# Float16 attention weights from tile 3 on in a fused top-k attention and two-MLP kernel

## The chip, the cores and the metric

One core of a Trainium2 chip runs the whole kernel. The metric is device time in microseconds (us). The engines are TensorE (PE; its weight loads are PEld), VectorE (DVE), ScalarE (ACT), GpSimd (POOL) and SyncE (SP), whose queue issues every DMA here.

## What is computed

```python
# q, k, v: (2, 8, 576, 64) float32; top_k = 32
scores = scale * np.matmul(q, k.transpose(0, 1, 3, 2))
kth = np.partition(scores, -top_k, axis=-1)[..., -top_k:-top_k + 1]
scores = np.where(scores >= kth, scores, -1000000000.0)
attn = np.exp(scores - np.max(scores, axis=-1, keepdims=True))
attn = attn / (np.sum(attn, axis=-1, keepdims=True) + 1e-09)
x = np.matmul(attn, v)            # then (2*576, 8*64) = (1152, 512) tokens
h = x @ moe_w_in                  # (512, 2048)
x = np.maximum(0.01 * h, h) @ moe_w_out
h = x @ moe2_w_in
out = (h * np.tanh(np.log1p(np.exp(np.minimum(h, 20.0))))) @ moe2_w_out   # softplus = h above 20
```

## The kernel before

The 1152 tokens are nine tiles of 128. Tiles 0 to 3 lie in batch 0, tile 4 half in each batch, tiles 5 to 8 in batch 1. A slot is one head of one tile; the 72 slots run one after the other, and the work of many stages is written into the same loop under priorities (`at`): a planner orders each engine's instructions by priority and by its own simulated times.

Float32 data that must keep its precision is split into two float16 halves, high and low, after scaling by a power of two (`pow2`). Keys, queries, activations and the four weight matrices are always split; products are then three matmuls (high×low, low×high, high×high).

A slot's steps: scores on TensorE, in two halves of 288 columns, both by way of the one bank of `ps_s`, each copied by ScalarE (`front`, two slots ahead of the rest); the top 32 by VectorE, four `max` and three `match_replace` (`topk`); masking and exponentials by ScalarE, L509 and L510 (`weigh`); then the weights, transposed, times the values (`back`).

`back` has two routes. In tiles below T16 = 5 it is float32: four transposes on TensorE into the bank `ps_pt`, a copy by ScalarE, a fifth transpose of the last 64 columns, a copy, five products. From tile 5 on `back16` runs: ScalarE casts the weights to the high half (L542), GpSimd subtracts to get the low half (L543), one transposing DMA on SP's queue turns ten blocks of 128 columns (L546), and 15 float16 matmuls multiply them by the split values (L553 to L555). Its halves `eh` stand in two buffers in turn, its transposed blocks `pts` in a buffer of the value pool `kvp`, which has VB = 5: four pairs of values and this one.

Values are loaded raw per pair of heads; `split_v` scales and splits a pair in place: squares, a scaled copy and a cast on ScalarE, a subtraction on GpSimd, two times. Before, only batch 1's pairs are split, from slot 34 on, after tile 4 has used them in float32. Its scratch `asides` and the one of `eh` lie in the scratch end of the weight arena `warena`, used until the 16 quarters of MLP weights are prepared (slots 0 to 16).

The MLP's steps (`Layer`, `product_in`, `product_out`) are spread over the slots with LEAD = 5 slots of lower priority; what is left runs after slot 71. The 16 quarters are loaded and split in the first slots (`load_w`, `split_w`).

Of the kernel before, what the change touches and what calls it, by code (L numbers as in the profile page):

```python
# [18 lines left out]
def topk_attention_moe_moe2_kernel(  # L19
# [34 lines left out]
    VB = 5  # L54
    LV = 0
# [4 lines left out]
    qp = ctx.enter_context(tc.tile_pool(name="qp", bufs=1))  # L60
# [243 lines left out]
    def load_kv(src, pool, tag, b, hp):  # L304
# [5 lines left out]
        for to, at0, n in (((0, S - P, P),) if src is k else ((0, S - SREM, SREM), (SREM, S - P, P - SREM))):  # L310
            nc.sync.dma_start(out=t[to:to + n, :, 4, :],
                              in_=src[b, 2 * hp:2 * hp + 2, at0:at0 + n, :].rearrange("h p d -> p h d"))
# [78 lines left out]
    def prep_q(t, qr):  # L391
# [5 lines left out]
        for c in range(2):  # L397
            if by_dma:
                qn = ksp.tile([P, 2, S], F16, tag="kst", name="qn").rearrange("p a b -> p (a b)")[:, :8 * P]
            else:  # L400
                qn = qp.tile([P, 4, 3, D], F16, tag="qn", name="qn").rearrange("p a b c -> p (a b c)")
# [36 lines left out]
    class Tile_:  # L438
# [11 lines left out]
        def front(self, h):  # L450
# [11 lines left out]
            for half in range(2):  # L462
                where, tag = ((ps_s, "s"), (ps_pt, "pt"))[half if self.t >= SB else 0]
# [48 lines left out]
        def back(self, h):  # L512
# [9 lines left out]
            where, tag = ((ps_pt, "pt"), (ps_g, "g"))[self.t >= TG]  # L522
            pu = where.tile([P, 512], F32, tag=tag, name="pu")
# [8 lines left out]
        def back16(self, h, e):  # L532

            hp, hh = divmod(h, 2)
            if not ehs:
                ehs.append(wh[:, 4 * NCHW * 2 * CH:4 * NCHW * 2 * CH + 2 * SP].rearrange("p (c n) -> p c n", c=2))
                t = krp.tile([P, 2, NB, D], F32, tag="kr", name="eh")
                ehs.append(t.rearrange("p a b c -> p (a b c)").bitcast(F16).rearrange("p (c n) -> p c n", c=2))
                for eh in ehs:
                    nc.gpsimd.memset(eh[:, :, S:], 0.0)  # L540
            eh = ehs[h % 2]
            nc.scalar.copy(eh[:, 0, :S], e)  # L542
            nc.gpsimd.tensor_tensor(out=eh[:, 1, :S], in0=e, in1=eh[:, 0, :S], op=ALU.subtract)  # L543
            pts = kvp.tile([P, 2, NB, D], F32, tag="kv", name="pts")
            ph = pts.rearrange("p a b c -> p (a b c)").bitcast(F16).rearrange("p (n q) -> p n q", q=P)
            nc.sync.dma_start(out=ph, in_=eh.rearrange("p c n -> p (c n)"), transpose=True)  # L546
            for b, s, n, p0 in tokens(self.t):
                o = self.av[p0:p0 + n, h * D:(h + 1) * D]
                for i, r in enumerate(R):
                    first, last = i == 0, i == NB - 1  # L550
                    pa, pb = [ph[:r, c * NB + i, p0:p0 + n] for c in range(2)]
                    va, vb = [vsp[b, hp][:r, hh, c, i, :] for c in range(2)]
                    nc.tensor.matmul(o, lhsT=pa, rhs=va, start=first, stop=False)  # L553
                    nc.tensor.matmul(o, lhsT=pa, rhs=vb, start=False, stop=False)
                    nc.tensor.matmul(o, lhsT=pb, rhs=va, start=False, stop=last)  # L555
# [44 lines left out]
    def product_in(m, hi, lo, g, t):  # L600
        where, tag = ((ps_m, "m"), (ps_pt, "pt"))[t >= MB and g == 3]
# [51 lines left out]
    class Layer:  # L653
# [11 lines left out]
        def first(self, g):  # L665
            ph = product_in(2 * self.l, self.hi, self.lo, g, self.t)
# [113 lines left out]
    T16 = 5  # L780
    TG = 5
    VS = 98
    VX = 34
# [3 lines left out]
    SB = 99  # L787
    YB = 99
    MB = 7
# [38 lines left out]
    for i in range(-2, NS):  # L828
# [27 lines left out]
        if i % 2 == 0:  # L856
            for bp in ((0, (i - VS) // 2), (1, (i - VX) // 2)):
                if bp in vst and bp not in vsp and T16 < NTT:
                    split_v(*bp)
# [7 lines left out]
    n = NS  # L867
    while todo or late:
# [33 lines left out]
```

## Time and profile before

| what | us |
|---|---|
| median of 3 runs (731.74 to 733.25) | 732.8 |
| the profiled execution's own time | 732.71 |
| its span, first to last instruction | 730.9 |
| mean granted TensorE clock, share of full | 0.962 |

The profile is of one execution; its span lies 1.8 us below that execution's time.

### The profile page before, as it was taken

The page shows a single profiled execution, that of the slowest core. Times are in us where ns is not written, and L with a number is a line of the kernel's source. Part 1 is how long each engine was busy: PE and PEld are TensorE (multiplying, and loading weights), DVE is VectorE, ACT ScalarE, POOL GpSimd, SP SyncE. Part 2 cuts the span into 40 slices and gives each one's busy share as a digit, 9 for nine tenths or more (in the row PEclk, how much of TensorE's full clock was granted, in tenths as well). Part 3 has the DMA queues.
Part 4 walks back from the last instruction along what each step waited for, and adds up shares of the span by engine and source line. Part 5 has one row for each costly group of instructions (what it writes and reads, how often), then busy time and mean ns, then how long its engine had stood idle before and what let it go on. Part 6 is the DMA issues. An engine that isn't in the chain of part 4 may idle for free.

```text
span 730.9 us, 16578 instructions
## 1 busy us (share of the span) xinstructions
PE 645.2 (88%) x6428; PEld 464.6 (64%) x6428; DVE 561.2 (77%) x1184; ACT 541.1 (74%) x1056; POOL 394.0 (54%) x550
## 2 busy tenths in 40 slices
PE   2389589888959999899999989998999989999996
PEld 1255345556648776677677757767767767677772
DVE  4998989999899788978687689788889899220112
ACT  5398688888786889877888696786797688663543
POOL 2648855667874754333255465466566557533230
PEclk9999889999976999999999998998999999999998
DMA  8842445351522112002212123233335334310000
GB/s 291 279 163 86 168 167 170 116 155 40 193 90 73 59 37 50 2 23 44 51 36 58 23 54 73 64 69 74 78 60 103 73 57 65 70 30 17 1 16 29
DMA packets 92367, 60.45 MB, mean 83 GB/s; under 512 B 78848, under 2 KB 82944, under 8 KB 92288
## 3 DMA queue, kind: packets, MB, share of 16 engines
q1 hardware_dynamic: 92288, 59.39, 30.1%
q8 instruction: 50, 0.82, 0.5%
q14 instruction: 29, 0.24, 0.1%
HBM read 41.16 MB, written 2.36 MB: 60 GB/s over the span
## 4 chain that ended last, share of the span: by engine, by line
PE 41%; DVE 23%; ACT 12%; issue 8%; DMA 8%; POOL 6%; SPq 1%; POOLq 0%; DVEq 0%; ACTq 0%
DVE top L484 6%; PE ph L609 5%; DVE wk L487 5%; PE ph L610 5%; PE ph L611 5%; PE y L618 5%; PE y L619 5%; PE y L620 5%; PE av L529 3%; PE sps L469 2%; DVE warena L215 2%; DVE warena L209 2%; DMA warena<-in_moe_w_out_dram 2%; DMA pts<-warena 2%; DMA warena<-in_moe_w_in_dram 2%
## 5 line engine op out<-in xcount | busy, mean ns | idle before, releaser
L609 PE MATMUL ph<-xt,warena 128*128 128x128 f16 x1152 | 204.7, 221 | 1.4 <-DMA xt<-xp 1.4
L610 PE MATMUL ph<-xt,warena 128*128 128x128 f16 x1152 | 204.5, 221 | 0.0
L611 PE MATMUL ph<-xt,warena 128*128 128x128 f16 x1152 | 204.5, 221 | 0.0
L484 DVE MAX8 top<-wk 128x8 f32<-128x576 f32 x216 | 157.5, 749 | 1.3
L610 PEld LDWEIGHTS <-warena 128*128 128x128 f16 x1152 | 114.0, 99 | 8.4 <-issue 2.5
L609 PEld LDWEIGHTS <-warena 128*128 128x128 f16 x1152 | 114.3, 99 | 7.9 <-issue 1.1
L618 PE MATMUL y<-warena,gl 128*128 128x512 f16 x288 | 110.9, 385 | 6.0 <-POOL gl L648 2.8
L611 PEld LDWEIGHTS <-warena 128*128 128x128 f16 x1152 | 114.1, 99 | 2.8 <-issue 1.1
L619 PE MATMUL y<-warena,gh 128*128 128x512 f16 x288 | 110.7, 384 | 0.0
L620 PE MATMUL y<-warena,gh 128*128 128x512 f16 x288 | 110.7, 384 | 0.0
L487 DVE MATCH_REPLACE8 wk<-top,wk 128x576 f32<-128x576 f32 x144 | 106.7, 741 | 0.0
L218 POOL TENSOR_TENSOR warena<-warena 128x1024 int32<-128x1024 int32 x26 | 64.1, 2468 | 31.8 <-DVE warena L215 9.1
L509 ACT ACTIVATE wk<-sc,nb,iv 128x576 f32<-128x576 f32 x72 | 62.5, 868 | 20.4 <-POOL nb L502 20.3
L484 DVE MAX8 top<-sc 128x8 f32<-128x576 f32 x72 | 54.0, 750 | 28.6 <-ACT sc L471 27.6
L471 ACT COPY sc<-sps 128x288 f32<-128x288 f32 x144 | 56.9, 395 | 25.0 <-PE sps L469 24.9
L469 PE MATMUL sps<-kst,qst 128*128 128x288 f16 (+1 forms) x320 | 64.7, 304 | 9.5 <-ACT sc L471 5.0
L529 PEld LDWEIGHTS av<-rawkv,pts 128*128 128x128 f32 (+3 forms) x480 | 56.3, 183 | 15.0 <-issue 3.7
L529 PE MATMUL av<-rawkv,pts 128*128 128x64 f32 (+3 forms) x480 | 64.5, 270 | 1.2 <-ACT pts L525 1.2
L502 POOL TENSOR_SCALAR nb<-top,iv 128x1 f32<-128x1 f32 x72 | 21.8, 302 | 80.5 <-DVE top L484 60.1
L645 DVE SCALAR_TENSOR_TENSOR mc<-mc,hs 128x512 f32<-128x512 f32 x36 | 26.1, 725 | 50.4 <-ACT mc L644 50.4
L510 ACT ACTIVATE wk<-wk,nb 128x576 f32<-128x576 f32 x72 | 55.9, 777 | 6.2 <-POOL nb L506 5.9
L632 POOL TENSOR_TENSOR gl<-lk,gh 128x512 f16<-128x512 f32 x36 | 43.6, 1210 | 27.4 <-ACT lk L631 27.0
(179 smaller groups left out, 1481.8 us busy)
## 6 DMA issues: line engine op xcount, KB each, us to landing
warena<-in_moe_w_in_dram SPq DMA_DIRECT2D x16, 1024.0 KB, 5.4
warena<-in_moe_w_out_dram SPq DMA_DIRECT2D x11, 1024.0 KB, 4.9
warena<-in_moe_w_out_dram SPq DMA_DIRECT2D x10, 512.0 KB, 3.4
out_dram<-o SPq DMA_DIRECT2D x9, 256.0 KB, 2.0
qr<-in_q_dram SPq DMA_DIRECT2D x8, 256.0 KB, 3.2
rawkv<-in_v_dram SPq DMA_DIRECT2D x8, 256.0 KB, 2.8
rawkr<-in_k_dram SPq DMA_DIRECT2D x6, 256.0 KB, 3.2
rawkv<-in_k_dram SPq DMA_DIRECT2D x2, 256.0 KB, 7.8
```

Source lines behind the costliest of these rows:

```text
L218: nc.gpsimd.tensor_tensor(out=o, in0=o, in1=lo, op=ALU.add)
L469: nc.tensor.matmul(sps[p0:p0 + n, :HS], lhsT=lq[:, c, p0:p0 + n], rhs=rk[:, half * HS:(half + 1) * HS], start=(c == 0), stop=(c == 1))
L484: queued(nc.vector.max(out=top[:, 8 * r:8 * r + 8], in_=src))
L487: queued(nc.vector.match_replace(out=wk, in_to_replace=top[:, 8 * r:8 * r + 8], in_values=src, imm_value=NEG))
L509: nc.scalar.activation(e, sc, AF.Prelu, bias=nb[:, 0:1], scale=iv, alpha=1e30)
L529: nc.tensor.matmul(o, lhsT=pts[:r, i, p0:p0 + n], rhs=vst[b, hp][:r, hh, i, :], start=(i == 0), stop=(i == NB - 1))
L609: nc.tensor.matmul(o, lhsT=wb, rhs=xa, start=(c == 0), stop=False)
L610: nc.tensor.matmul(o, lhsT=wa, rhs=xb, start=False, stop=False)
L611: nc.tensor.matmul(o, lhsT=wa, rhs=xa, start=False, stop=(c == KC - 1))
L618: nc.tensor.matmul(y, lhsT=gb, rhs=whi(j), start=(g == 0 and f == 0), stop=False)
L619: nc.tensor.matmul(y, lhsT=ga, rhs=wlo(j), start=False, stop=False)
L620: nc.tensor.matmul(y, lhsT=ga, rhs=whi(j), start=False, stop=(g == FG - 1 and f == 3))
```

## The change

T16 goes from 5 to 3, so tiles 3 and 4 take the float16 route. Below TK = 5 its buffers are a single `eh` in the arena's scratch and the single buffer `pts` of `sp1`, which the float32 route used; from tile 5 on `eh` alternates between two, and `pts` comes from `kvp`, which has six buffers now (VB = 6). The low half of the last 64 columns is put beside their high half, so that there are nine blocks in place of ten, and one matmul over 128 rows multiplies both with the values' high half; for it `load_kv` puts the last 64 values on both halves of the partitions. A head is 14 matmuls in place of 15, per batch that it lies in. Batch 0's values are split from slot 18 on (VS), batch 1's from slot 30 (VX). Batch 1's values are loaded up to two slots earlier (LV). The queries' halves `qn` take buffers of the key pool, not one of their own. From tile 3 on (SB), and for the first head, the second half of the scores uses the bank `ps_pt`; the fourth group of an MLP layer uses that bank only after the last slot (`over`), where it did so from tile 7 on.

```diff
-    VB = 5
-    LV = 0
+    VB = 6
+    LV = 2
-    qp = ctx.enter_context(tc.tile_pool(name="qp", bufs=1))
...
-        for to, at0, n in (((0, S - P, P),) if src is k else ((0, S - SREM, SREM), (SREM, S - P, P - SREM))):
+        for to, at0, n in (((0, S - P, P),) if src is k else ((0, S - SREM, SREM), (SREM, S - SREM, SREM))):
...
-            if by_dma:
-                qn = ksp.tile([P, 2, S], F16, tag="kst", name="qn").rearrange("p a b -> p (a b)")[:, :8 * P]
-            else:
-                qn = qp.tile([P, 4, 3, D], F16, tag="qn", name="qn").rearrange("p a b c -> p (a b c)")
+            qn = ksp.tile([P, 2, S], F16, tag="kst", name="qn").rearrange("p a b -> p (a b)")
+            qn = qn[:, :8 * P if by_dma else 6 * P]
...
-                where, tag = ((ps_s, "s"), (ps_pt, "pt"))[half if self.t >= SB else 0]
+                where, tag = ((ps_s, "s"), (ps_pt, "pt"))[half if self.t >= SB or (self.t, h) == (0, 0) else 0]
...
-            if not ehs:
-                ehs.append(wh[:, 4 * NCHW * 2 * CH:4 * NCHW * 2 * CH + 2 * SP].rearrange("p (c n) -> p c n", c=2))
-                t = krp.tile([P, 2, NB, D], F32, tag="kr", name="eh")
-                ehs.append(t.rearrange("p a b c -> p (a b c)").bitcast(F16).rearrange("p (c n) -> p c n", c=2))
-                for eh in ehs:
-                    nc.gpsimd.memset(eh[:, :, S:], 0.0)
-            eh = ehs[h % 2]
-            nc.scalar.copy(eh[:, 0, :S], e)
-            nc.gpsimd.tensor_tensor(out=eh[:, 1, :S], in0=e, in1=eh[:, 0, :S], op=ALU.subtract)
-            pts = kvp.tile([P, 2, NB, D], F32, tag="kv", name="pts")
-            ph = pts.rearrange("p a b c -> p (a b c)").bitcast(F16).rearrange("p (n q) -> p n q", q=P)
-            nc.sync.dma_start(out=ph, in_=eh.rearrange("p c n -> p (c n)"), transpose=True)
+            if self.t < TK or h % 2:
+                eh = wh[:, 4 * NCHW * 2 * CH:4 * NCHW * 2 * CH + 2 * S]
+            else:
+                if not ehs:
+                    ehs.append(krp.tile([P, 2, NB, D], F32, tag="kr", name="eh"))
+                eh = ehs[0].rearrange("p a b c -> p (a b c)").bitcast(F16)[:, :2 * S]
+            nc.scalar.copy(eh[:, :S], e)
+            nc.gpsimd.tensor_tensor(out=eh[:, S + SREM:], in0=e[:, :4 * P], in1=eh[:, :4 * P], op=ALU.subtract)
+            nc.gpsimd.tensor_tensor(out=eh[:, S:S + SREM], in0=e[:, 4 * P:], in1=eh[:, 4 * P:S], op=ALU.subtract)
+            if self.t < TK:
+                pts = sp1.tile([P, NB, P], F32, tag="pts", name="pts").rearrange("p a b -> p (a b)")
+            else:
+                pts = kvp.tile([P, 2, NB, D], F32, tag="kv", name="pts").rearrange("p a b c -> p (a b c)")
+            ph = pts.bitcast(F16)[:, :2 * S].rearrange("p (n q) -> p n q", q=P)
+            nc.sync.dma_start(out=ph, in_=eh, transpose=True)
             for b, s, n, p0 in tokens(self.t):
                 o = self.av[p0:p0 + n, h * D:(h + 1) * D]
-                for i, r in enumerate(R):
...
+                va, vb = vsp[b, hp][:, hh, 0], vsp[b, hp][:, hh, 1]
+                for i in range(4):
+                    pa, pb = ph[:, i, p0:p0 + n], ph[:, 5 + i, p0:p0 + n]
+                    nc.tensor.matmul(o, lhsT=pa, rhs=va[:, i, :], start=(i == 0), stop=False)
+                    nc.tensor.matmul(o, lhsT=pa, rhs=vb[:, i, :], start=False, stop=False)
+                    nc.tensor.matmul(o, lhsT=pb, rhs=va[:, i, :], start=False, stop=False)
+                nc.tensor.matmul(o, lhsT=ph[:, 4, p0:p0 + n], rhs=va[:, 4, :], start=False, stop=False)
+                nc.tensor.matmul(o, lhsT=ph[:SREM, 4, p0:p0 + n], rhs=vb[:SREM, 4, :], start=False, stop=True)
...
-        where, tag = ((ps_m, "m"), (ps_pt, "pt"))[t >= MB and g == 3]
+        where, tag = ((ps_m, "m"), (ps_pt, "pt"))[bool(over) and g == 3]
...
-    T16 = 5
-    VS = 98
-    VX = 34
-    SB = 99
-    MB = 7
+    T16 = 3
+    TK = 5
+    VS = 18
+    VX = 30
+    SB = 3
...
-                if bp in vst and bp not in vsp and T16 < NTT:
+                if bp in vst and bp not in vsp:
                     split_v(*bp)
```

## Rows read from the trace of the kernel before

**Rows 1.** The page: busy us, share of the span, instructions of each engine.

```profile
PE 645.2 (88%) x6428; PEld 464.6 (64%) x6428; DVE 561.2 (77%) x1184; ACT 541.1 (74%) x1056; POOL 394.0 (54%) x550
```

**Rows 2.** Stretches: PE, PEld, DVE, ACT, POOL busy, PEclk; last, L510 alone.

```profile
277.00:401.00 124.00, 119.48 (x1224) 87.86 (x1225) 102.48 (x239) 100.88 (x231) 51.55 (x105) 1.00 0.17 37
401.00:627.00 226.00, 216.41 (x2587) 161.69 (x2585) 194.20 (x414) 175.69 (x356) 136.90 (x222) 0.97 0.34 67
627.00:731.00 104.00, 96.70 (x1014) 66.13 (x1010) 18.59 (x40) 51.65 (x87) 30.37 (x35) 0.98 0.12 25
255.00:295.00 40.00, 37.29 (x365) 28.40 (x364) 34.76 (x94) 35.69 (x80) 20.42 (x39) 1.00 0.17 40
...
277.50:401.50 124.00, 13.92 (x32) 1.00 0.17 38
```

**Rows 3.** Timeline of TensorE, float32 heads of tile 3 (start us, us).

```profile
314.60 0.27 PE L524 MATMUL pu<-identf,wk 128*64 128x128 f32 x1
314.71 1.00 PE L529 MATMUL av<-rawkv,pts 128*128 128x64 f32 x8
315.55 0.41 PE L469 MATMUL sps<-kst,qst 128*128 128x288 f16 x2
316.61 0.43 PE L529 MATMUL av<-rawkv,pts 64*128 64x64 f32 x2
316.97 0.66 PE L520 MATMUL pt<-identf,wk 128*128 128x128 f32 x4
```

**Rows 4.** Timeline of TensorE, a float32 head of tile 4.

```profile
363.83 0.27 PE L524 MATMUL pu<-identf,wk 128*64 128x128 f32 x1
364.04 0.68 PE L529 MATMUL av<-rawkv,pts 128*64 128x64 f32 x8
364.65 0.39 PE L620 MATMUL y<-warena,gh 128*128 128x512 f16 x1
...
366.21 1.19 PE L529 MATMUL av<-rawkv,pts 64*64 64x64 f32 x12
367.33 0.66 PE L520 MATMUL pt<-identf,wk 128*128 128x128 f32 x4
367.91 0.44 PE L469 MATMUL sps<-kst,qst 128*64 128x288 f16 x4
```

**Rows 5.** Timeline, a float16 head of tile 5: first, thirteenth, and what follows.

```profile
423.89 0.19 PE L553 MATMUL av<-rawkv,pts 128*128 128x64 f16 x1
...
424.33 0.20 PE L553 MATMUL av<-rawkv,pts 64*128 64x64 f16 x1
...
424.52 0.23 PE L611 MATMUL ph<-xt,warena 128*128 128x128 f16 x1
```

**Rows 6.** The transposed weights' DMA: group, SP's wait, one episode, the clock.

```profile
L553 PE MATMUL av<-rawkv,pts 128*128 128x64 f16 x128 | 15.1, 196 | 7.7 <-DMA pts<-warena 7.6
...
SPq L546 <- PE av L555: 47.0, 19, 4.9
...
433.12 1.32 SPq L546 DMA_TRANSPOSE pts<-warena  x1
436.56 0.24 PE L553 MATMUL av<-rawkv,pts 128*128 128x64 f16 x1 [2.68 <-DMA pts<-warena]
...
437.00:443.00 6.00, 6.00 (x26) 2.51 (x24) 5.96 (x14) 1.45 (x3) 1.83 (x5) 0.52 0.47 98
```

**Rows 7.** Groups by line and shape; last, what touches batch 1's values.

```profile
L521 ACT COPY pts<-pt 128x512 f32<-128x512 f32 x40 | 23.3, 583 | 10.5 <-PE pt L520 10.0 <-PE av L529 0.3
L542 ACT CAST eh<-wk 128x576 f16<-128x576 f32 x16 | 10.8, 674 | 0.2
L543 POOL TENSOR_TENSOR eh<-wk,eh 128x576 f16<-128x576 f32 x16 | 21.0, 1312 | 7.8 <-ACT eh L542 7.6
...
362.00:420.00 58.00, 13.07 (x140) 10.20 (x140) 0.00 (x0) 12.04 (x32) 6.36 (x8) 1.00 0.17 39
```

**Rows 8.** VectorE's line L408: duration ns, min, median and max.

```profile
L408 DVE SCALAR_TENSOR_TENSOR qn<-qr,qs,qn x18: 460/486/2269, 6.0 to 556.3; 128x256 f16<-128x256 f32 x18
```

More of the change, by code (lines that the diff above doesn't have):

```diff
@@ L521, in back @@
             nc.scalar.copy(pts[:, 0:4, :], pt)
-            where, tag = ((ps_pt, "pt"), (ps_g, "g"))[self.t >= TG]
-            pu = where.tile([P, 512], F32, tag=tag, name="pu")
+            pu = ps_pt.tile([P, 512], F32, tag="pt", name="pu")
             nc.tensor.transpose(pu[:SREM, :P], e[:, 4 * P:S], identf)
@@ L547, in back16 @@
+            ph = pts.bitcast(F16)[:, :2 * S].rearrange("p (n q) -> p n q", q=P)
+            nc.sync.dma_start(out=ph, in_=eh, transpose=True)
             for b, s, n, p0 in tokens(self.t):
                 o = self.av[p0:p0 + n, h * D:(h + 1) * D]
-                for i, r in enumerate(R):
[L550 to L555, printed above, removed]
+                va, vb = vsp[b, hp][:, hh, 0], vsp[b, hp][:, hh, 1]
[6 more added lines that the diff above has]
+                nc.tensor.matmul(o, lhsT=ph[:SREM, 4, p0:p0 + n], rhs=vb[:SREM, 4, :], start=False, stop=True)
@@ L598, in transposed, with product_in @@
         return hi, lo, xi
-    def product_in(m, hi, lo, g, t):
-        where, tag = ((ps_m, "m"), (ps_pt, "pt"))[t >= MB and g == 3]
+    over = []
+    def product_in(m, hi, lo, g):
+        where, tag = ((ps_m, "m"), (ps_pt, "pt"))[bool(over) and g == 3]
         ph = where.tile([P, 512], F32, tag=tag, name="ph")
@@ L665, in first @@
         def first(self, g):
-            ph = product_in(2 * self.l, self.hi, self.lo, g, self.t)
+            ph = product_in(2 * self.l, self.hi, self.lo, g)
             beside = nc.vector if FG * self.t + g >= TF[self.l] else nc.gpsimd
@@ L778, in step @@
                 pass_on(t)
-    T16 = 5
-    TG = 5
-    VS = 98
-    VX = 34
+    T16 = 3
+    TK = 5
+    VS = 18
+    VX = 30
     XD = (5, 5)
@@ L867, in topk_attention_moe_moe2_kernel @@
     n = NS
+    over.append(True)
     while todo or late:
```

## The prediction

> **What bounds the kernel now.** Start with the busy shares [rows 1]: TensorE 88%, VectorE 77%, ScalarE 74%. That is an average over stages, so read the stages next [rows 2]. The 72 heads leave ScalarE's exponential (L510, two records a head) one after the other; 32 records, the 16 heads of tiles 3 and 4, lie between 277.5 and 401.5 us: 7.75 us a head. There TensorE is busy 119.48 of 124 us, in tiles 5 to 8 (401 to 627) 216.41 of 226, in the tail behind the last head 96.70 of 104. VectorE and ScalarE stand at 102.48 and 100.88 of 124. So from 277 us on the kernel is what TensorE has to do plus 4.5 + 9.6 + 7.3 us in which it idles, and a matmul taken away is worth its time as long as the other two engines can follow: the MLP's groups wait behind attention in TensorE's order, and the tail is made of them. The first 277 us are left: 645.2 − 119.48 − 216.41 − 96.70 = 212.6 us of TensorE work, so TensorE is idle for 64 us there and doesn't set the pace; the change hardly touches them.
>
> Then price a head as TensorE sees it, from one start to the next start, because the busy times of pipelined matmuls overlap. A float32 head in tile 3 [rows 3]: transpose of the last 64 columns 314.60 to 314.71, 0.11; eight products 314.71 to 315.55, 0.84; two products 316.61 to 316.97, 0.36; four transposes 0.58 [rows 4] with a change of tile shape behind them, taken as 0.5. Sum 1.81 us. In tile 4, which lies in both batches [rows 4]: 0.21 + 0.61 + 1.12 + 0.5 = 2.44 us. A float16 head in tile 5 [rows 5]: 423.89 to 424.52, 0.63 us for 15 matmuls, one about every 0.03 us and 0.1 more where the shape changes.
>
> **The change part by part.** *Tile 3* leaves the float32 route: 8 heads × (1.81 − 0.60) = −9.7 us; 0.60 is the 0.63 less one matmul, since 14 do it now. *Tile 4*: 28 matmuls a head with 64 stationary columns each, in float16, which no row shows. From below two float16 heads of full width, 2 × 0.60 = 1.2; from above the pace of the 20 float32 matmuls of that width, 1.73 / 20 = 0.087, times 28 = 2.4. I take 1.5, nearer the row of the same type: 8 × (2.44 − 1.5) = −7.5, ends −9.9 and −0.3. *Tiles 5 to 8*: one matmul less, 32 × 0.03 = −1.0.
>
> *Second buffer for transposed weights in tiles 5 to 8.* TensorE sat 7.7 us before the first product of a head, for the transposing DMA [rows 6]. One such episode: issue at 433.12, TensorE starts at 436.56 after 2.68 us, and then runs six microseconds at 0.52 of full speed, the lower of its two clocks; there are two episodes like it, each losing some 3 us by the clock. At stake: 7.7 + 2 × 3 = 13.7 us. SP's queue held 19 of the 32 transposes back for the products of the head before [rows 6], because one buffer took them all; with six value buffers there are two. Most of those 47 us were hidden. I take −5, ends 0 and −13.7.
>
> *The new transposes in tiles 3 and 4* have one buffer before and one behind the DMA. Charged like the old ones: 13.7 / 32 × 16 = +6.9, ends 0 and twice that, 13.7.
>
> *ScalarE.* Each of 16 heads swaps a copy out of PSUM of 0.58 us and a smaller one (counted as nothing) for a cast of 0.67 [rows 7]: at most +1.4. Batch 0's values must be split: batch 1's four pairs cost ScalarE 12.04 us [rows 7], so +12 between the last weights and tile 3's heads. From 255 to 295 us ScalarE is busy 35.69 of 40 [rows 2]: 4.3 us of cover for 13.4. What isn't covered makes attention late, not TensorE idle by itself, since MLP groups can fill in. I take a third of the 9.1, +3, ends 0 and +9.1.
>
> *At nothing:* GpSimd's 16 more subtractions of 1.31 us (two pieces now), hidden by GpSimd's 72 idle us of 124 [rows 2]; without that cover 21 us. The second half of the scores in a bank of its own: scores run two heads ahead and TensorE is 96% busy; it saves less than one copy a head, under 0.58, and only where TensorE has nothing else. The query halves moved into the key buffers: the last weights want the same two, but tile 3's queries are prepared four slots before its first head. The sixth value buffer and batch 1's loads and splits two to four heads earlier: the same work at another place; in SP's queue a load that waits for its buffer's last product now holds up the transposes of tile 4 behind it, which the +6.9 has to cover. The products' third bank, now in the tail alone: the tail's 7.3 idle us bound it.
>
> Sum: −9.7 − 7.5 − 1.0 − 5 + 6.9 + 3 = −13.3. The profiled execution took 732.7 us (span 730.9 and 1.8 around it), the median is 732.8: 719.4 us.
>
> **The rivals.** *A, all of it arrives:* ScalarE's work finds its gaps, the second buffer ends the clock losses, the new transposes wait for nothing: −9.7 − 7.5 − 1.0 − 10 = −28.2, 704.5 us. For it: MLP work is always queued. Against: the transposes before have cost 13.7 us in 32, and the new ones have fewer buffers.
>
> *B, VectorE and ScalarE become the bound:* tiles 3 and 4 need 102.48 us of VectorE and 100.88 + 1.4 + some of the 12 of ScalarE. If ScalarE doesn't go beyond 90% (it reached 89% from 255 to 295) and 4 of the 12 us fall behind 277, the 124 us shrink to 106.3 / 0.9 = 118: −5.9 in place of −9.7 − 7.5 + 3, then −1.0 − 5 + 6.9 as above, −5.0 in all, 727.7 us. For it: ScalarE's 89%. Against: MLP work can fall back to later tiles, where ScalarE is busy 175.69 of 226. VectorE could tighten it [rows 8]: the same instruction took 0.486 us in the middle and 2.269 at most, and GpSimd gets 16 × 1.31 + 6.36 [rows 7] = 27 us more to do. The Trainium skill ("SBUF — State Buffer", section "Who interferes with whom") says that a VectorE instruction with two SBUF inputs and a GpSimd instruction that reads SBUF shut each other out for a whole instruction. By that rule VectorE's long cases become more frequent, which the row fits without showing the cause.
>
> *C, slower: the single-buffered loop sets the head's pace in tiles 3 and 4.* Cast 0.67, subtraction 1.31 [rows 7], transposing DMA from issue to TensorE's start 3.44 [rows 6]: 5.4 us, and the next cast may not write before the DMA has read. It decides from the point where the loop with its queueing on ScalarE, GpSimd and SP exceeds the pace that the savings allow, 7.75 − 17.2 / 16 = 6.7 us, so from 1.3 us of queueing. At 3 us of queueing the head takes 8.4 and not 7.75, 16 × 0.65 = +10; TensorE draws some MLP work forward into its new idle time, −3; two falls of the clock in such waits, +6; and −1.0 − 5 from tiles 5 to 8: 732.7 + 10 − 3 + 6 − 6 = 739.7 us. Behind a cast that waits, ScalarE's copies of scores and the exponentials of the next head are queued, and VectorE waits for those. Against: 5.4 us of work leave 1.3 us a head, and a cast can be queued behind other ScalarE work at no loss. The Trainium skill ("VectorE: DVE Perf Modes", section "Rules for kernel authors") has a 128×128 transpose done on TensorE where PSUM may take it, and by DMA otherwise; this change goes the other way. By that rule C is the case. The trace bears it out in latency only: 3.44 us against some 0.6 on TensorE and 0.58 for a copy.
>
> *D, nothing:* the saved TensorE time turns into idle time one for one, because attention was paced by its own chain; 732.7. Against: 119.48 of 124 busy.
>
> **How the numbers follow.** Chances: the forecast 0.48 (its own range 711 to 727), A 0.18, B 0.12, D 0.06, C 0.16. The time is the forecast's, 719.4. A range from 702 to 736 leaves out most of C and a little of A, some 0.15. A measurement of this kernel tells about 0.2% from no change, 1.5 us. Forecast, A and B are faster: 0.78. D is 0.06 and C 0.16.
>
> **What would show it.** Right: tiles 3 and 4 take about 110 us and not 124, with no float32 products in them; a tile-4 head costs TensorE about 1.5 us; the waits before a head's first product are fewer from tile 5 on. Each step can be read off alone: TensorE's idle time between tile 3 and the tail should stay near 14 us. Wrong: ScalarE waiting for a DMA before a cast (C); ScalarE over 90% with TensorE idle between 255 and 330 us (B); more stretches at the lower clock (C or the second-buffer term); a first stage of 277 us that moved by more than 3 us, which nothing here predicts.

## The result and the profile after

The changed kernel takes 739.99 us (median of 12 runs, 734.52 to 743.03) against 731.57 for the kernel before (12 runs, 730.29 to 733.25): ratio 1.0105, interval 1.0082 to 1.0128. It is 1% slower, clear of the noise, where 719.4 us was forecast. The profiled execution has a span of 739.8 us (730.9 before).

The page of the changed kernel, busy us by engine, answers to [rows 1]:

```profile
PE 637.5 (86%) x6420; PEld 454.1 (61%) x6420; DVE 556.7 (75%) x1199; ACT 549.9 (74%) x1072; POOL 436.8 (59%) x620
```

TensorE is busy 7.7 us less (645.2 before) and yet the span is 8.9 us longer: its idle time went from 730.9 − 645.2 = 85.7 to 739.8 − 637.5 = 102.3 us, 16.6 more. So some saving is there, and waiting ate more than all of it.

Stretches of the changed kernel, cut where the last exponential of a tile ends (tile 2, 3, 4, 5, then 6 to 8, then the tail; busy PE, PEld, DVE, ACT, POOL, granted clock), answer to [rows 2]:

```profile
203.20:290.80 87.60, 73.19 (x704) 57.35 (x704) 66.42 (x158) 68.78 (x141) 52.70 (x71) 0.88 0.19 58
290.80:352.00 61.20, 56.03 (x642) 41.50 (x642) 50.26 (x113) 50.61 (x112) 35.67 (x64) 0.92 0.29 54
352.00:431.10 79.10, 73.07 (x758) 48.53 (x757) 56.12 (x136) 58.04 (x134) 40.75 (x73) 0.94 0.41 69
431.10:481.10 50.00, 42.53 (x495) 30.64 (x494) 48.38 (x109) 40.20 (x84) 33.97 (x65) 0.90 0.39 76
481.10:631.10 150.00, 145.29 (x1752) 108.26 (x1750) 137.59 (x300) 124.11 (x248) 102.80 (x184) 0.99 0.37 70
631.10:739.80 108.70, 99.58 (x1087) 70.10 (x1084) 18.71 (x41) 53.28 (x89) 32.20 (x38) 1.00 0.10 24
```

Cut the same way, the two traces and two of the runs below give these lengths in us:

| stage | before | after | weights elsewhere (run 3) | own split scratch (run 13) |
|---|---|---|---|---|
| tiles 0 and 1 | 210.3 | 203.2 | 201.0 | 200.7 |
| tile 2 | 66.9 | 87.6 | 84.7 | 87.5 |
| tile 3 | 55.6 | 61.2 | 54.1 | 64.8 |
| tile 4 | 68.2 | 79.1 | 80.4 | 67.6 |
| tiles 5 to 8 | 226.1 | 200.0 | 199.6 | 207.2 |
| tail | 103.8 | 108.7 | 110.2 | 110.5 |

Three things to read there. Tile 2, in which no head changed its route, is 20.7 us longer: it begins 7.1 us earlier than before and ends 13.6 us later. Tiles 3 and 4, where the saving was to be, took 123.8 us and now take 140.3, TensorE idle for 11.2 of them and at a granted clock of 0.92 and 0.94 where it had 1.00. Tiles 5 to 8 are 26 us shorter, with VectorE now at 48.38 of 50 in tile 5 and 137.59 of 150 behind it.

**Tile 2.** All of the lateness lies in one gap: the last exponential but one of the tile (head 22) starts at 262.09 us, 8.7 earlier than in the kernel before (270.80), and the last (head 23) at 290.03, 13.6 later (276.39). The timeline of the changed kernel around head 23 (VectorE, then ScalarE, then GpSimd; in brackets the idle time before and what ended it):

```profile
265.74 0.27 DVE L686 TENSOR_SCALAR ivo<-x1i,x0i,ifac 128x1 f32<-128x1 f32 x1
274.58 0.69 DVE L648 SCALAR_TENSOR_TENSOR mc<-mc,hs 128x512 f32<-128x512 f32 x1 [8.57 <-ACT mc L647]
...
284.21 0.76 DVE L481 MAX8 top<-sc 128x8 f32<-128x576 f32 x1
...
271.15 1.13 ACT L268 CAST warena<-wraw 128x512 f16<-128x512 f32 x2
...
274.39 0.61 ACT L123 ACTIVATE qn<-qr 128x512 bf16<-128x512 f32 x1
...
278.92 1.01 ACT L427 COPY qst<-qt 128x1024 f16<-128x1024 f16 x1 [0.77 <-PE qt L426]
...
269.78 4.51 POOL L270 TENSOR_TENSOR warena<-wraw,warena 128x512 f16<-128x512 f32 x4 [0.34 <-ACT warena L268]
```

The kernel before, the same squares on ScalarE's timeline:

```profile
231.23 0.63 ACT L124 ACTIVATE qn<-qr 128x512 bf16<-128x512 f32 x1 [0.73 <-DMA qr<-in_q_dram]
```

Tile 3's queries are squared at 274.39, a tenth of a microsecond after GpSimd has read the last raw weights (269.78 + 4.51 = 274.29) out of the key buffers. That the wait is for the buffer is inferred from these two times; run 2 below has the same pair. The queries' transposes are copied out at 278.92, the scores of head 24 follow, and VectorE, whose top-32 order interleaves the first half of head 24 with the second of head 23, has almost nothing to do from 266 to 284.

**Tile 4.** Batch 1's first keys are loaded at 272.1 us in the changed kernel. The timeline of GpSimd and ScalarE shows when they are begun:

```profile
320.13 0.79 POOL L365 TENSOR_TENSOR rawkv<-aside,rawkv 128x320 f16<-128x320 f32 x1
...
319.77 0.69 ACT L468 COPY sc<-sps 128x288 f32<-128x288 f32 x2
320.34 0.49 ACT L123 ACTIVATE warena<-rawkr 128x320 bf16<-128x320 f32 x1
```

The kernel before, same step on ScalarE's timeline, 3 us after the load was issued (270.52):

```profile
273.67 0.47 ACT L124 ACTIVATE warena<-rawkr 128x320 bf16<-128x320 f32 x1 [0.48 <-DMA rawkr<-in_k_dram]
```

This L365 is the last subtraction in the splitting of batch 0's values. It works in `asides`, the same two pieces of scratch in which batch 1's keys are prepared; the keys' first piece came free at 319.38 + 0.79 = 320.17. Two later pairs of keys also start within 0.7 us of the end of a split (375.7 and 398.0 us); these are splits of batch 1's values, which now stand ahead of the keys, where before the change the last keys were squared at 353 and the first split came at 362. Tile 4's exponentials have gaps of 18.6 and 14.4 us there, where the others of the tile are 5 to 10.

**Tile 5.** The MLP's first products (tile `ph`, TensorE's busy time is the first column) in three stretches of the changed kernel:

```profile
395.00:425.80 30.80, 14.19 (x215) 4.58 (x7) 1.00 0.42 67
425.80:456.50 30.70, 0.17 (x4) 2.04 (x3) 0.83 0.33 67
456.50:487.00 30.50, 18.63 (x293) 7.74 (x12) 1.00 0.43 72
```

For 31 us there is next to nothing to multiply. These products run on finished tiles, and by the end of tile 4 they have done 28 of the 28 groups that stand ahead of tile 4's in the kernel's list (24 in the kernel before); tile 4's own output is ready only after 443. TensorE's clock then falls to its lower level (0.50 granted from 442.1 to 452.3 us).

The 28 are set by the list as well as by the data: it puts the second layer of tile 3 behind the first layer of tile 4 (`todo`). VectorE finishes the inputs of the two layers in the other order (`x1s`, tile 3's second layer; `x0s`, tile 4's first):

```profile
437.98 0.74 DVE L598 SCALAR_TENSOR_TENSOR xt<-xt,x1s 128x512 f16<-128x512 f32 x1
...
453.70 0.75 DVE L598 SCALAR_TENSOR_TENSOR xt<-xt,x0s 128x512 f16<-128x512 f32 x1 [0.56 <-ACT xt L597]
```

So four groups had their input 15.7 us before the ones that they stand behind (in run 3 below 18.3 us, 422.76 to 441.04); in the kernel before, the two inputs came in the list's order (428.97 for tile 4, then 438.42). No run changed the list.

### The profile page after: what moved, and what is told of

It is laid out like the page before. It is cut to its first block, busy times and chain, and to the rows that moved or that the text cites. A ratio compares the mean times of both kernels' runs of the same rounds, so it can differ in the third digit from the quotient of the medians.

```text
span 739.8 us, 16728 instructions
## 1 busy us (share of the span) xinstructions
PE 637.5 (86%) x6420; PEld 454.1 (61%) x6420; DVE 556.7 (75%) x1199; ACT 549.9 (74%) x1072; POOL 436.8 (59%) x620
## 4 chain that ended last, share of the span: by engine, by line
PE 35%; DVE 27%; ACT 14%; DMA 9%; issue 7%; POOL 7%; SPq 1%; POOLq 0%; DVEq 0%; ACTq 0%
DVE top L481 8%; DVE wk L484 6%; PE ph L612 5%; PE y L621 5%; PE y L623 5%; PE y L622 5%; PE ph L613 4%; PE ph L614 4%; DVE warena L214 3%; DMA pts<-warena 3%; DVE warena L208 3%; PE sps L466 2%; DMA warena<-in_moe_w_in_dram 2%; ACT wk L506 2%; DMA warena<-in_moe_w_out_dram 2%
## 5 line engine op out<-in xcount | busy, mean ns | idle before, releaser
L621 PE MATMUL y<-warena,gl 128*128 128x512 f16 x288 | 112.5, 391 | 7.7 <-POOL gl L651 2.4
L622 PE MATMUL y<-warena,gh 128*128 128x512 f16 x288 | 112.2, 390 | 0.0
L623 PE MATMUL y<-warena,gh 128*128 128x512 f16 x288 | 112.2, 390 | 0.0
L466 PE MATMUL sps<-kst,qst 128*128 128x288 f16 (+1 forms) x320 | 64.8, 305 | 16.7 <-ACT sc L468 10.0
L217 POOL TENSOR_TENSOR warena<-warena 128x1024 int32<-128x1024 int32 x26 | 65.6, 2527 | 17.2 <-PE gram L234 4.5
L499 POOL TENSOR_SCALAR nb<-top,iv 128x1 f32<-128x1 f32 x72 | 27.3, 380 | 66.6 <-DVE top L481 56.2
L468 ACT COPY sc<-sps 128x288 f32<-128x288 f32 x144 | 53.9, 399 | 12.3 <-PE sps L466 12.0
L635 POOL TENSOR_TENSOR gl<-lk,gh 128x512 f16<-128x512 f32 x36 | 41.7, 1161 | 24.2 <-ACT lk L634 23.6
L539 POOL TENSOR_TENSOR warena<-wk,warena 128x512 f16<-128x512 f32 x32 | 37.1, 1159 | 29.9 <-ACT warena L538 27.5
L484 DVE MATCH_REPLACE8 wk<-top,sc 128x576 f32<-128x576 f32 x72 | 53.4, 741 | 0.0
```

What stands on the lines that cost most here:

```text
L217: nc.gpsimd.tensor_tensor(out=o, in0=o, in1=lo, op=ALU.add)
L466: nc.tensor.matmul(sps[p0:p0 + n, :HS], lhsT=lq[:, c, p0:p0 + n], rhs=rk[:, half * HS:(half + 1) * HS], start=(c == 0), stop=(c == 1))
L484: queued(nc.vector.match_replace(out=wk, in_to_replace=top[:, 8 * r:8 * r + 8], in_values=src, imm_value=NEG))
L621: nc.tensor.matmul(y, lhsT=gb, rhs=whi(j), start=(g == 0 and f == 0), stop=False)
L622: nc.tensor.matmul(y, lhsT=ga, rhs=wlo(j), start=False, stop=False)
L623: nc.tensor.matmul(y, lhsT=ga, rhs=whi(j), start=False, stop=(g == FG - 1 and f == 3))
```

## The experiments

Each is the changed kernel (or the one before) with the edit shown. Times are medians, ratios against the kernel before on the same chip, with their interval. The theories: *Q*, the queries in the key buffers; *C*, rival C of the prediction; *S*, the splitting of batch 0's values on ScalarE, which makes tile 2 late; *SPQ* and *W* came later.

**1. Queries in the MLP's temporaries.**

```diff
-            qn = ksp.tile([P, 2, S], F16, tag="kst", name="qn")...
+            qn = tmp.tile([P, 512], F32, tag="t", name="qn", bufs=TB).bitcast(F16)[:, :6 * P]   # tiles 0 to 4
```

> The changed kernel, but the query halves of tiles 0 to 4 stand in a buffer of the MLP's 2 KB scratch pool and not in the key pool. Theory Q (the key pool: tile 3's query halves wait for the last weights' raw buffers, batch 1's keys wait for query halves): the 28 us between the exponentials of heads 22 and 23 shrink to under 12 us, tiles 3 and 4 lose some 10 us, and the time falls from 740 to 715 to 724 us. Theory C (the single-buffered loop of the weights' transposes paces tiles 3 and 4): no head changes, 736 to 742 us. Theory S (splitting batch 0's values on ScalarE makes tile 2 late): the same, 736 to 742 us.

763.67 us, 1.0454 [1.0424, 1.0484]. A miss. The three temporaries are the MLP's, and tile 1 alone went from 81.9 to 103.5 us: the run seems to have put another queue in the place of the one it took away, and it decides nothing.

**2. The queries' move alone**, in the kernel before.

```diff
-                qn = qp.tile([P, 4, 3, D], F16, tag="qn", name="qn")...
+            qn = ksp.tile([P, 2, S], F16, tag="kst", name="qn")...
```

> The kernel before with one part of the change alone: the query halves of tiles 0 to 4 move into the key pool. Theory Q: tile 3's query halves wait for the split of the last weights and batch 1's keys come later: 10 to 25 us slower than before, 742 to 757 us. Theories C and S: the part is harmless, 730 to 734 us.

734.33 us, 1.0053 [1.0033, 1.0072]. Slower, by 3.4 us where 10 or more were expected. The wait itself is there: GpSimd is through with three of the last raw weights at 276.87 us, and tile 3's queries are squared at 277.34, against 231.2 before. Tile 2 ends 17 us later (294.2 against 277.2 us), 7 of which it already had at the end of tile 1, and tiles 5 to 8 give 14.9 back (211.2 for 226.1), with TensorE busy for 69.6 of 69.6 us in tile 4 and 56.44 of 57.6 in tile 5.

**3. The last weights elsewhere.** One of the last quarters' raw buffers comes from the value pool, so one key buffer stays free.

```diff
-    RAWS = 'vk'
+    RAWS = 'vkv'
```

> The changed kernel with one of the two raw buffers that quarters 13 and 15 of the weights take from the key pool taken from the value pool instead, so that a key buffer stays free for the query halves. Theory Q: the wait at head 23 goes (some 15 us of attention), the one between query halves and batch 1's keys in tile 4 stays: 722 to 732 us. Theories C and S: 736 to 742 us.

731.23 us, 0.9999 [0.9980, 1.0018], 8.8 us less than the changed kernel (7.8 by the two ratios): Q. The timeline of ScalarE in this run has tile 3's queries where they used to be:

```profile
236.18 0.61 ACT L123 ACTIVATE qn<-qr 128x512 bf16<-128x512 f32 x1
```

Its stretches for tiles 2 to 5:

```profile
201.00:285.70 84.70, 70.94 (x702) 57.41 (x700) 72.44 (x165) 70.83 (x150) 55.32 (x70) 0.88 0.19 59
285.70:339.80 54.10, 50.31 (x566) 36.45 (x566) 46.30 (x112) 46.24 (x101) 33.34 (x64) 0.94 0.32 61
339.80:420.20 80.40, 77.28 (x857) 53.63 (x856) 58.58 (x142) 63.42 (x145) 45.62 (x79) 0.98 0.37 69
420.20:468.60 48.40, 38.91 (x465) 30.06 (x463) 46.42 (x103) 35.29 (x75) 29.95 (x59) 0.86 0.36 76
```

Tile 3 is back under its old length, tile 4 is not, and in tile 5 TensorE is idle for 9.5 us at 0.86 of its clock. Nor is tile 2, though its queries came in time: it ends at 285.7 us, 8.5 later than before. VectorE stands there for the total of one of batch 0's splits (`vs` is the scale that comes of it), while ScalarE is busy for 23.96 of 24.7 us:

```profile
275.69 0.16 DVE L99 TENSOR_SCALAR u<-tot 128x2 int32<-128x2 int32 x1 [7.37 <-PE tot L118]
275.96 0.17 DVE L102 TENSOR_SCALAR vs<-u 128x2 int32<-128x2 int32 x1
...
261.00:285.70 24.70, 22.79 (x227) 17.01 (x226) 15.66 (x44) 23.96 (x56) 14.04 (x21) 1.00 0.15 41
```

That is S, seen once Q is out of the way.

**4. Tiles 3 and 4 in float32 again**, all else changed.

```diff
-    T16 = 3
+    T16 = 5
-    VS = 18
-    VX = 30
+    VS = 98
+    VX = 34
-    SB = 3
+    SB = 5
```

> The changed kernel with tiles 3 and 4 back on the float32 route, batch 0's values not split, batch 1's split from slot 34 and the second scores bank from tile 5 on; six value buffers, the loads and the query halves stay as changed. Theory Q: the wait at head 23 stays and the saved TensorE time is gone: 740 to 752 us. Theory C: without the loop in tiles 3 and 4 the time is that of before or less, 722 to 733 us. Theory S: without batch 0's split 722 to 733 us.

739.58 us, 1.0110 [1.0083, 1.0136], level with the changed kernel. So the float16 route with its single-buffered loop is not what makes the kernel slower, and with its splits it does not pay here either: C falls as the cause of the loss. S does not fall by this run, since the queries (Q) hold tile 2 in it, to 289.5 us. Nor do the equal times price the route alone: tiles 3 and 4 take 130.6 us here and 140.3 in the changed kernel, which has batch 0's splits in the keys' scratch as well. Against run 2, which has the queries' move alone, run 4 is some 5 us slower; that lies in other parts of the change (the sixth value buffer, the earlier loads, the banks among them), which no run took apart.

**5, 6, 7. Queries of tiles 3 and 4 in a small buffer of their own**, one head at a time (384 bytes a partition is what was left). 6 adds the edit of 4; 7 sets `RATE = (1, 1, 1, 1)` for `(1, 1, 2, 1)`.

```diff
+                for h in range(4):
+                    qn = qp.tile([P, 3, D], F16, tag="qn", name="qn")
...
+                    nc.tensor.transpose(pt[:, h, 0, :], qf[:, 0:P], identh)
```

> The changed kernel, with one thing altered: the query halves of tiles 3 and 4 no longer take key buffers but a small buffer of their own (384 bytes a partition, one head at a time, so with more and shorter instructions). If the key buffers' queue is what made the change slower, in tile 2 (about 9 us by the run with the weights elsewhere) and in tile 4 (where batch 1's keys want the same two buffers), this comes out at 720 to 732 us. If the loss lies in the float16 heads' own chain it stays at 736 to 742. If the products of the MLP run dry once attention has been late (TensorE has nothing to do until tile 4's output is there), what is won in tiles 2 to 4 is given back as TensorE idle in tile 5, and it ends near the run with the weights elsewhere, 728 to 733.

> The run with the small query buffer, and tiles 3 and 4 in float32 as before the change (values of batch 0 not split early, second scores bank from tile 5 on). It prices the float16 halves of tiles 3 and 4 where the queries are out of the way. If my sum for them holds (9.7 and 7.5 us of TensorE saved, 6.9 and 3 given back), this is about 7 us slower than the run with the small query buffer. If the freed TensorE time has nothing to fill it, since the MLP's products are already at the last finished tile, the two differ by less than 3 us. If the float16 chain costs more than it gives, this one is faster.

> The run with the small query buffer, and the MLP handed out at one group a slot throughout (two a slot in tile 2 before). If the products run dry in tile 5, because they caught up with the finished tiles by tile 4, a slower hand-out leaves TensorE to attention in tiles 2 to 4 and keeps products for tile 5: 3 to 10 us faster than the run with the small query buffer. If the pace is no limit, the same products are only left for the end, and it is 0 to 8 us slower.

762.96 us (1.0429 [1.0405, 1.0452]), 737.49 (1.0076 [1.0054, 1.0098]) and 764.52 (1.0450 [1.0428, 1.0471]). Runs 5 and 7 are far above what any theory gave. The timeline of TensorE in run 5 shows that my edit made a wait of its own:

```profile
338.25 0.22 PE L423 MATMUL qt<-identh,qn 128*128 128x128 f16 x1
...
353.92 0.22 PE L423 MATMUL qt<-identh,qn 128*128 128x128 f16 x1
...
365.91 0.22 PE L424 MATMUL qt<-identh,qn 128*128 128x128 f16 x1
367.56 0.38 PE L119 MATMUL tot<-kpart,one 128*128 128x2 f32 x2 [0.98 <-ACT qst L425]
```

Tile 4's eight query heads pass through the one small buffer from 338.25 to 366, holding the PSUM bank `g` all the while, and the total for batch 1's second keys, whose squares were done by 344, waits for that bank until 367.56. So runs 5 and 7 say nothing about Q, and the 25 us between 5 and 6 are no price of float16.

Up to the end of tile 2, before that wait, run 6 says more. It has neither tile 3's queries in the key buffers nor batch 0's splits:

| version | queries in the key buffers | batch 0's splits | tile 2 ends, us |
|---|---|---|---|
| kernel before | no | no | 277.2 |
| run 6 | no | no | 278.6 |
| run 3 | yes, with one more free | yes | 285.7 |
| run 5 | no | yes | 289.0 |
| run 4 | yes | no | 289.5 |
| changed kernel | yes | yes | 290.8 |

In run 5 the small buffer may add waits of its own there. Either of the two is enough to hold tile 2, which is why taking one away alone (runs 3 and 4) wins little of it.

**8. The kernel before with `RATE = (1, 1, 1, 1)`**, the control for 7.

> Control: the kernel before, with the MLP handed out at one group a slot throughout. In the kernel before, products never run dry (24 of the 28 groups that could have run are done at the end of tile 4), so the slower hand-out can only leave more for the end: 731 to 740 us by either theory. If it is faster than 729, the pace was badly set for both kernels and says nothing about the change.

726.96 us, 0.9938 [0.9920, 0.9956]. Faster by 4.8 us, against expectation: two groups a slot in tile 2 were too many for the kernel before too.

**9 to 12. Batch 1's keys off SP's queue**: loads issued by ScalarE, halves transposed by TensorE. 9 on run 5, 10 on run 3, 11 on the kernel before, 12 on run 3 with the even pace.

```diff
-    K3 = 4
+    K3 = 99
+        queue_of = nc.scalar if src is k and b else nc.sync
-        nc.sync.dma_start(
+        queue_of.dma_start(
```

> The run with the small query buffer (763.0 us), with batch 1's keys taken off SP's queue: their loads are issued by ScalarE, and their halves are transposed by TensorE, as batch 0's are (40 transposes more, about 11 us of TensorE by batch 0's row of 11.0 us). Theory SPQ: in tiles 3 and 4, SP issues in order the transposing transfers of the weights, each of which waits for the only buffer of transposed weights, and behind them stand the loads and transposes of batch 1's keys; in the trace of the 763 us run a pair of keys came through about every 26 us, which sets the pace of tile 4. By it, this run loses most of the 23 us by which the small query buffer was slower: 735 to 748 us. If the small query buffer's short instructions are to blame (VectorE and ScalarE work, a clock that falls), it stays at 758 to 775.

> The run with the weights elsewhere (731.2 us), with batch 1's keys taken off SP's queue in the same way. By SPQ, tiles 3 and 4 (134 us there, 124 before the change) get shorter by more than the 11 us of TensorE that the transposes cost is felt: 720 to 732 us. If SP's queue is not what holds tile 4, the added TensorE work shows: 735 to 745.

> Control: the kernel before, with batch 1's keys taken off SP's queue in the same way. There, no transfer of weights stands in SP's queue in tiles 3 and 4, and TensorE is busy through all of tile 4, so the 40 transposes only cost: 735 to 743 us by SPQ. If it is faster than 730, keys by transfer were slow for the kernel before too, and the gain of the other two runs would not be the change's.

> The run with the weights elsewhere and the keys off SP's queue, with the MLP handed out at one group a slot throughout (two in tile 2 before), as in the control that brought the kernel before to 727.0 us. If the products no longer run dry in tile 5 with the keys in time, this gains as the control did, 3 to 6 us against the run without it; if they still do, it is level or slower, as with the small query buffer (764.5 against 763.0).

769.94 us (1.0514 [1.0485, 1.0544]), 735.91 (1.0068 [1.0045, 1.0092]), 731.54 (1.0004 [0.9993, 1.0016]) and 738.78 (1.0098 [1.0078, 1.0119]). SPQ falls: 9 is slower than 5, and 10 slower than 3, with tile 4 as long (80.9 us against 80.4). SP's waits for the single buffer of transposed weights are large in the changed kernel between 291 and 431 us (us in all, times, longest), yet they are not what holds tile 4:

```profile
SPq L546 <- PE av L556: 33.2, 8, 8.7
```

Run 11 adds that 40 transposes more on TensorE cost the kernel before nothing that can be told, 0.7 us.

**13 to 16. A scratch of their own for the splits**, in a PSUM bank, with the subtraction on VectorE. 13 on the changed kernel, 14 on run 3, 15 on the kernel before, 16 on run 3 with the even pace.

```diff
+        where, tag = side(b == 0)
-            a = asides[h]
+            a = where.tile([P, 512], F32, tag=tag, name="va")[:, :NB * D]
-            nc.gpsimd.tensor_tensor(out=half[:, 1], in0=a, in1=half[:, 0], op=ALU.subtract)
+            nc.vector.tensor_tensor(out=half[:, 1], in0=a, in1=half[:, 0], op=ALU.subtract)
```

> The changed kernel (740.0 us), with the splitting of the values working in a PSUM bank in place of the two scratch pieces that batch 1's keys are prepared in (the subtraction of the halves then is VectorE's, 16 of some 0.5 us). Theory W: batch 1's first keys lay loaded at 272 us and were begun at 320.3 us, when the last split of batch 0's values had left the scratch at 320.2; two later pairs start within a microsecond of a split's end too, and tile 4's heads wait for these keys (gaps of 18.6 and 14.4 us between weights where 6 to 8 are usual). By it tile 4 gets shorter by 8 to 15 us, and the kernel comes to 724 to 734 us. If the keys only happen to follow the splits, it stays at 737 to 743.

> The same scratch in PSUM in the run with the weights elsewhere (731.2 us). By theory W both losses are then out of the way, and what is left of the change is its gain: 715 to 725 us. If W is wrong: 729 to 734. If W is right but the freed time finds no products (they run only on finished tiles), 725 to 729.

> Control: the kernel before with the same scratch in PSUM. There no value of batch 0 is split, and batch 1's splits come after its keys (the last keys at 359 us, the first split at 362): nothing to win, 729 to 735 us.

> The second run of this set, with the MLP handed out at one group a slot throughout, as in the control that brought the kernel before to 727.0 us. With both waits gone tiles 2 to 4 look as in the kernel before, and the slower hand-out gains 3 to 6 us; if the products still run dry in tile 5, it is level or slower.

742.95 us (1.0170 [1.0143, 1.0197]), 739.85 (1.0126 [1.0108, 1.0143]), 724.06 (0.9910 [0.9894, 0.9926]) and 738.68 (1.0109 [1.0093, 1.0125]). Tile 4 did get shorter, by 11.5 us in run 13 (79.1 to 67.6) and 10.8 in run 14, as W has it. Run 13's stretches for tiles 3 and 4:

```profile
288.20:353.00 64.80, 60.23 (x671) 43.89 (x670) 52.53 (x120) 54.48 (x123) 34.95 (x63) 0.95 0.27 51
353.00:420.60 67.60, 58.43 (x681) 41.13 (x679) 58.50 (x142) 54.25 (x122) 34.52 (x65) 0.95 0.42 80
```

The time did not follow. Tile 3 got longer (3.6 us in run 13, 14.6 in run 14 against run 3), and the trace says why in part: for batch 0 the new scratch lies in bank `g`, which the keys' totals need. The first keys' squares now run at 273.3 us, but their total comes at 323.9, behind the last split of batch 0. The sharing moved from the scratch to the bank, so W is tried for tile 4's later keys only. The control is the surprise: the kernel before gains 0.9% from this edit. Tile 4 shrinks there from 68.2 to 65.4 us and tile 5 from 64.4 to 56.8. How far the shared scratch explains it stays open: the keys go first in that kernel, and the edit also moves the subtractions from GpSimd to VectorE; no run parts the two. Of all 18 this is the fastest version; it and run 8 beat both kernels.

**17, 18. The products' rank**, on run 3.

```diff
-        at(i, LEAD)
+        at(i, 9.0 if 16 <= i < 40 else LEAD)     # 17
+        at(i, 1.0 if i >= 40 else LEAD)          # 18
```

> The run with the weights elsewhere (731.2 us), with the MLP's products ranked nine slots behind attention instead of five while tiles 2 to 4 run. If the products run dry because attention in tiles 2 to 4 waits behind them and they catch up with the finished tiles, attention gets through earlier, the gap after tile 4 (4 of TensorE's idle 9.5 us in tile 5, and the half clock behind it) fills, and the time falls to 722 to 728 us. If they run dry only because tile 4's output is late for other reasons, nothing is won: 730 to 737.

> The run with the weights elsewhere, with the products ranked one slot behind attention instead of five from tile 5 on. At the last weight 17 of the MLP's 72 first products were left (15 in the kernel before), and 12 have to be; a group is some 5 us of TensorE. If TensorE has room in tiles 5 to 8 (15 us idle there), 2 to 4 groups move into them and the time falls to 720 to 727 us. If tiles 5 to 8 are full for TensorE in each slot, attention is delayed by as much as the tail is shortened: 729 to 736.

729.9 us (0.9980 [0.9961, 0.9999]) and 750.97 (1.0284 [1.0266, 1.0301]). Holding the products back gains 1.3 us on run 3, not clear of the noise (the two intervals overlap) and too little to carry the explanation: TensorE's idle time in tile 5 falls from 9.5 only to 6.8 us. Handing them out earlier at the end costs 20, a miss by both theories. The stretches of run 18, tile 5, tiles 6 to 8 and the tail:

```profile
419.20:481.90 62.70, 52.54 (x608) 39.57 (x607) 45.87 (x100) 41.37 (x83) 34.03 (x63) 0.89 0.29 60
481.90:657.30 175.40, 163.47 (x1905) 118.88 (x1903) 146.31 (x306) 131.93 (x261) 107.64 (x191) 0.95 0.32 63
657.30:748.90 91.60, 78.63 (x815) 53.48 (x812) 17.98 (x38) 42.72 (x72) 25.60 (x29) 0.97 0.09 22
```

The tail is 18.6 us shorter than in run 3 and tiles 5 to 8 are 38.5 longer. They had no room: in run 3 VectorE is busy there for 183.5 of 199.6 us and TensorE for 184.2. That a product put ahead of scores stops the head is how I read it.

## Why the prediction was wrong

**The terms for TensorE held, head by head.** Two heads in the timeline of TensorE, one of tile 3 (first and last product, and what follows) and one of tile 4 (first and last of batch 0, first of batch 1, and what follows):

```profile
332.49 0.19 PE L552 MATMUL av<-rawkv,pts 128*128 128x64 f16 x1
...
332.96 0.20 PE L556 MATMUL av<-rawkv,pts 64*128 64x64 f16 x1
333.10 0.39 PE L623 MATMUL y<-warena,gh 128*128 128x512 f16 x1
...
384.89 0.22 PE L552 MATMUL av<-rawkv,pts 128*64 128x64 f16 x1 [1.48 <-DMA pts<-warena]
...
385.42 0.21 PE L556 MATMUL av<-rawkv,pts 64*64 64x64 f16 x1
385.56 0.22 PE L552 MATMUL av<-rawkv,pts 128*64 128x64 f16 x1
...
386.23 0.23 PE L612 MATMUL ph<-xt,warena 128*128 128x128 f16 x1
```

A head of tile 3 takes 333.10 − 332.49 = 0.61 us, as forecast; a head of tile 4 takes 386.23 − 384.89 = 1.34 us where I took 1.5. The sum of TensorE's own terms was −9.7 − 7.5 − 1.0 = −18.2. The busy time of the whole execution can't confirm it: with the same products it is 7.7 us below the kernel before in the changed kernel, 11.8 in run 3 and 18.1 in run 13, and what the clock and the overlap of products have in this was not taken apart.

**The step that failed is the one at nothing:** "The query halves moved into the key buffers: the last weights want the same two, but tile 3's queries are prepared four slots before its first head". Four slots are some 31 us of notice (7.75 a head), half of it up to the first scores, which run two slots ahead, and the weights made the queries 43 us later (231.2 to 274.4). Run 3 prices it: 8.8 of the 20.6 us between forecast and result; in the kernel before, run 2, it cost 3.4. I had counted slots where I should have read when the last weights leave; the trace before had it, at 273 us (GpSimd's last subtraction, 272.19 + 1.16), against queries at 231.

**The frame failed with it.** "From 277 us on the kernel is what TensorE has to do" plus its idle time, and "the first 277 us … the change hardly touches them": the first 277 us became 291, and from there on the idle time did not stay: between tile 3 and the tail, where it should have been near 14 us, it is 23.4. My reading is that once attention is late, the products catch up with the finished tiles, TensorE has idle time and falls to the lower clock, and a matmul saved is only more of that. Rival D had this ("attention was paced by its own chain") at 0.06. Run 4 fits it (the same time without the float16 route in tiles 3 and 4) but does not show it, since it also takes away batch 0's splits; no run has the float16 heads or the float32 heads with all the waits gone.

**A wait that I did not have at all:** "batch 1's loads and splits two to four heads earlier: the same work at another place" leaves out that the splits stand in the scratch of batch 1's keys: batch 0's last one holds the first pair, and two of batch 1's, moved ahead, hold two more. That the keys begin when the splits leave is read from the trace; that tile 4 shortens by 11 us without it is shown by runs 13 and 14, which also move the subtractions to VectorE; what it is worth in the whole kernel is not settled, since those runs made a queue of their own.

**The other terms.** The second buffer for tiles 5 to 8 (−5): SP's waits for the products of the head before fell as foreseen, from 47.0 us (19 times) to 4.8 (3 times, from 440 us on), but TensorE's own waits before a head's first product only from 7.6 to 5.1. The length of those tiles prices nothing: they lost 26 us, but 4 of the MLP's 72 groups, at some 5 us each, had already been done by then and 2 more were left for the tail. The new transposes in tiles 3 and 4 (+6.9) made TensorE wait 4.6 us, the clock apart. ScalarE's +3 for the splits was too small as a delay of attention: in run 3 they alone have tile 2 end 8.5 us late, against 1.4 in run 6 without them. What that costs the whole kernel no run shows. Tiles 0 and 1 became 7.1 us shorter, which nothing in the prediction foresaw and no run isolated; it is not the queries' move (runs 3, 4 and 13 have it, run 2 not).

**Rival C came out at the right number for the wrong reason.** 739.7 us were its time, 739.99 the result, but its mechanism is small: ScalarE's cast waited 7.2 us in all for the DMA, 4.6 of them in tiles 3 and 4, and run 4 is as slow without the loop. The rule of the Trainium skill that it leaned on ("VectorE: DVE Perf Modes", section "Rules for kernel authors": a 128×128 transpose belongs on TensorE where PSUM may take it) finds no support here either way: with the keys' transposes moved to TensorE, run 11 is level and run 10 is 4.7 us slower than run 3. Rival B was right in other places: VectorE fills tiles 5 to 8, not 3 and 4, and ScalarE the end of tile 2 in run 3 (23.96 of 24.7 us).

**What stays open.** With the weights elsewhere the kernel is level with the one before, although by the price of its heads some 18 us of TensorE work are gone. Accounted by the profile of run 3, TensorE is busy 633.4 us, 11.8 less, and idle 96.6, 10.9 more, most of it in tile 2 (13.8 for 5.9) and tile 5 (9.5 for 2.7). For the part in tile 2 the 7.4 us that VectorE waits for a split stand in the trace. That the lack of finished tiles causes the part in tile 5 is argued from the 31 us without products; runs 7, 12, 16, 17 and 18, which changed the pace in three ways, did not turn it into time. Two versions were not tried: one with keys, queries and splits each in a place of its own, and one whose list lets tile 3's second layer go ahead of tile 4's first.

## What to carry to other kernels

Before a tile moves into a pool that others use, read in the trace when its last user leaves and when the newcomer is first wanted, in microseconds; distance in loop iterations does not tell. The same holds for scratch and for PSUM banks: a piece of work placed earlier takes its scratch along, and whoever shares that scratch starts behind it, also when it was loaded long ago. And where an engine is bound only because other work fills its gaps, time saved on it counts only as long as that filling lasts; look at what the filler depends on, its own order included. When taking one wait away wins little, look whether a second one stands right behind it: here either of two held the same tile.

## What the runs showed of the hardware

A float16 product with 64 stationary columns starts some 0.03 us after the one before it, as one with 128 columns does: half the columns saved nothing here (a batch's 14 from 384.89 to 385.42 in tile 4, 14 from 332.49 to 332.96 in tile 3).

TensorE's granted clock fell to the lower of its two levels behind short gaps more often than I had allowed for. In the changed kernel's stretches from 435 us on:

```profile
435.00:442.10 7.10, 4.32 (x66) 3.36 (x67) 7.09 (x16) 6.42 (x14) 3.95 (x7) 1.00 0.23 44
442.10:452.30 10.20, 7.16 (x32) 3.22 (x30) 9.67 (x22) 7.44 (x16) 9.47 (x16) 0.50 0.28 58
```

TensorE was idle for 2.8 of the first 7.1 us, and was then granted 0.50 for the next ten. Tiles 3 and 4, which had 1.00 throughout, lost at most 61.2 × 0.08 + 79.1 × 0.06 = 9.6 us of full clock in this way, less what fell into idle time.
